# A new written order for the first ten cells: x's low parts copied between the halves by ScalarE, masks of five weight units in PSUM

## The chip, the cores and the metric

The kernel runs on one NeuronCore of one Trainium2 chip. The metric is device microseconds from the start to the end of one execution. Before the change three runs gave a median of 1227.36 us; two of them lie at 1226.69 and 1227.36, the third at 2097.7.

## The reference, cut to what matters

```python
# x: (2, 4096, 192), weight_gen: (2, 4096, 8, 7); all float32
w = softmax(weight_gen, axis=-1)                 # 7 weights for each token and head
out[b, s, h, g] = sum_k w[b, s, h, k] * x_pad[b, s + k, h, g]   # causal window of 7 tokens
x = out.reshape(8192, 192)
h = x @ w_in1;  x = where(h > 0, h, exp(min(h, 0)) - 1) @ w_out1    # 192 -> 2048 -> 192
h = x @ w_in2;  x = (h * clip(h + 3, 0, 6) / 6) @ w_out2            # 192 -> 2048 -> 192
```

All inputs are float32, and the products are made nearly exact: each operand is split into a high part (`h`) and a low rest (`l`), and three products of parts are added (high by high, high by low, low by high).

## The kernel before, in words

**Tiling.** The 8192 tokens are 16 blocks of 512. A cell is one block, one of the two layers and one eighth of the 2048 hidden columns, so a block has 8 cells per layer, and the kernel 256 cells in all. A cell n has a first product (18 pairs of matmuls with 64 rows each, into two of the four `h` banks of PSUM: `h00` and `h01` for even n, `h10` and `h11` for odd n), an activation on ScalarE (`act_a`, L556 and L557), a gate on VectorE (`gate`, L573), the rounding of the result to `gh` on ScalarE (L563), its rest `gl` on VectorE (L567), and a second product, which is issued with the first product of cell n + 3 into `acca` and `accb`. All matmuls of cells are recorded at L536.

**Weight units.** The weights of layer one are split on the chip, in 16 units of 384 columns (numbered 0 to 15; units 4, 6, 8, 10 and 12 to 15 belong to `w_out`, the others to `w_in`). A unit takes a mask step on ScalarE (`B`, L158), five integer steps on VectorE (`s0` to `s4` at L162, L165, L169, L174, L185, written C9.0 to C9.4 for unit 9), a rounding to the high part on ScalarE (`H`, L180), three matmuls that make the low part in a PSUM bank (`P`, L191 to L193), and the copy of that bank into the low weights (`L`, L198). The strings `masks` and `sums` name, per unit, where the steps' scratch lies and into which bank the three matmuls go: `x` is `aux`, `b` is `accb`, `a` and `c` are the two `acca`, `d` to `g` the banks `h00`, `h01`, `h10`, `h11`, and `-` an SBUF tile called `tr`.

**The window products.** The window sum of a block is made on GpSimd (`attention`, L290 and L299): 14 tensor operations on SBUF of about 1.5 to 2.7 us. They start when VectorE has scaled the block's softmax weights (L278).

**The written order.** Up to cell 9 nothing is scheduled by rule: the instructions are issued in the order of the string `SCRIPT`, and each engine executes its own in that order. `M3` there is the matmuls of cell 3, `x3` and `y3` the activations of its two banks, `X3` and `Y3` their gates, `R3` and `G3` the two rounding steps. `s1a`, `e1`, `s1b`, `s1c` and `sA`, `sE`, `sB`, `sC` are the softmax steps of blocks 1 and 2, the last of each with L278 and GpSimd's products behind it. `T1`, `J` and `j` transpose and split x of block 1. For block 0, `wh0` and `wh1` round x to `xh`, `wh2` and `wh3` copy `xh` between the partition halves on ScalarE (L348), and `wl0` and `wl1` make the rest `xl` on VectorE (L352). `wl1` also issues two DMAs on SyncE's queue that copy `xl` between the halves (L357), and then the loads of units 8 to 11. From cell 10 on, the loop at the end of the kernel sets the order, with a stream that spreads the weight units of layer two over the cells.

Of the kernel before, what the change touches and what calls it, by code (L numbers as in the profile page):

```python
# [8 lines left out]
F32 = mybir.dt.float32  # L9
# [8 lines left out]
def kernel(  # L18
# [20 lines left out]
    nc = tc.nc  # L39
# [19 lines left out]
    half = slice(0, HP), slice(HP, P)  # L59
# [268 lines left out]
    def prepare(m, i):  # L328
        X = xts[m, i] = {
            k: act.tile([P, 2, XN], F32R, tag=f"x{k}", name=f"x{k}") for k in "hl"}  # L330
        v = lambda t: t[:, 0].rearrange("p (h c) -> p h c", h=2)
        if m == 0:

            y, yd = ya.pop(i)
            ps = acca if i == 0 else (acca[i % 2], aux)
            for t, src in enumerate([y[:, t, 0:P] for t in range(TM)] + [yd[:, s] for s in range(2)]):
                for h, p in enumerate(half):
                    nc.tensor.transpose(ps[h][:, t * HP:(t + 1) * HP], src[p], ident[p, p])  # L338
            parts = [(ps[h][:, 0:XN // 2], (lambda h: lambda t: v(t)[:, h])(h)) for h in range(2)]
        else:  # L340
            parts = [(zin.pop(i)[:, 0:XN], lambda t: t[:, 0])]

        def cast(k):
            src, w = parts[k]
            nc.scalar.copy(w(X["h"]), src)  # L345

        def turn(a):
            nc.scalar.copy(X["h"][half[1 - a], 1], X["h"][half[a], 0].bitcast(F32))  # L348

        def rest(k):  # L350
            src, w = parts[k]
            nc.vector.tensor_tensor(w(X["l"]), src, w(X["h"]).bitcast(F32), op=ALU.subtract)  # L352

        def swap(keys, put):
            for k in keys:
                for a in range(2):
                    put(X[k][half[1 - a], 1].bitcast(F32), X[k][half[a], 0].bitcast(F32))  # L357

        def split():
            for k in range(len(parts)):  # L360
                cast(k)
            for k in range(len(parts)):
                rest(k)
            swap("hl", lambda o, t: later(1 if (m, i) == (0, 2) else 2, o, t))
        split.cast, split.turn, split.rest, split.swap = cast, turn, rest, swap
        return split

# [227 lines left out]
    def later(n, out, in_):  # L595

        if now is None or now >= len(cells) or now < BOOT and n == 0:
            nc.sync.dma_start(out, in_)
        else:
            waiting.append((now + n, out, in_))  # L600
# [8 lines left out]
    class Stream:  # L609
# [21 lines left out]
    BOOT = 10  # L631
    units = [(u[0], 0, int(u[1]), k) for k, u in enumerate("i0 i1 i2 i3 o0 i4 o1 i5 o2 i6 o3 i7 o4 o5 o6 o7".split())]
    banks = {"x": aux, "b": accb, "a": acca[0], "c": acca[1], "d": hset[0][0], "e": hset[0][1], "f": hset[1][0], "g": hset[1][1]}
    masks, sums = "xxbaccxcx----ccc", "xxbfbedgfedxcxxx"
    made = {}
    SCRIPT = """
        s1a B2 B1 C2.0 e1 C1.0 wh0 s1b wh1 wh2 wl0 s1c wh3 wl1 C2.1 B4 M0 C1.1 B3 C2.2 C4.0 H2 C1.2 C4.1 H1
        C1.3 C3.0 C1.4 C4.2 P1 x0 C3.1 C4.3 C3.2 L1 M1 C4.4 y0 C2.3 X0 B5 C2.4 B6 Y0 P2 x1 C5.0 C6.0 y1 C3.3
        C6.1 X1 L2 M2 H3 C3.4 R0 Y1 C5.1 P3 H4 C6.2 x2 G0 P4 y2 C5.2 C6.3 L3 C5.3 L4 M3 C6.4 C5.4 X2 B7 B8
        Y2 R1 C8.0 C7.0 H5 C8.1 H6 P5 C7.1 x3 C8.2 G1 P6 L5 B9 B10 C7.2 L6 M4 C8.3 H7 sA C10.0 sE X3 y3 C7.3  # L640
        C10.1 C9.0 H8 C8.4 R2 C7.4 Y3 P7 x4 C9.1 C10.2 P8 C9.2 L7 G2 H10 T1 L8 C10.3 y4 M5 C9.3 X4 C9.4 J
        C10.4 sB B12 H9 j B11 R3 Y4 P9 B13 sC C11.0 C12.0 G3 P10 L9 x5 C11.1 C12.1 C11.2 L10 M6 C13.0 H11
        C12.2 C13.1 H12 C11.3 x6 C13.2 C11.4 C13.3 R4 C12.3 C13.4 P11 y5 C12.4 X5 P12 G4 H13 L11 L12 Y5 B14
        X6 M7 R5 C14.0 C14.1 x7 G5 y6 X7 C14.2 P13 H14 C14.3 Y6 L13 M8 C14.4 y7 R6 Y7 B15 G6 x8 P14 R7 C15.0
        X8 L14 M9 C15.1 C15.2 H15 C15.3 C15.4 x9 G7 y8 P15 y9 Y8 X9 L15 Y9 R8 G8
    """

    groups = [("io"[n % 2], 1, n // 2) for n in range(2 * NQ)]
# [22 lines left out]
    with tc.manual_schedule():  # L671
        nc.vector.memset(three, 3.0)
        nc.scalar.activation(warm, three, AF.Exp)
        def make(k):
            made[k] = Unit(*units[k])
# [20 lines left out]
        c1, split = attention(1), {0: prepare(0, 0)}  # L696
# [29 lines left out]
        def special(t):  # L726
            if t == "T1":
                split[1] = prepare(0, 1)
            elif t in ("s1a", "e1", "s1b"):
                c1.pop(0)()  # L730
            elif t == "s1c":
                for s in c1:
                    s()
            elif t == "J":
                split[1].cast(0)
                split[1].cast(1)
            elif t == "j":
                split[1].rest(0)
                split[1].rest(1)
                split[1].swap("hl", nc.sync.dma_start)  # L740
            elif t[:2] == "wh":
                k = int(t[2])
                (split[0].turn if k > 1 else split[0].cast)(k % 2)
            elif t[:2] == "wl":
                split[0].rest(int(t[2]))
                if t == "wl1":
                    split[0].swap("l", nc.sync.dma_start)
                    for k in range(8, RAWS + 8):
                        make(k)
            else:  # L750
                if t == "sA":
                    softmax[2] = attention(2)
                softmax[2].pop(0)()
# [6 lines left out]
        for t in SCRIPT.split():  # L760
            if t[0] == "C":
                k, p = t[1:].split(".")
                getattr(made[int(k)], "s" + p)()
            elif t[0] in plain and t[1:].isdigit():
                plain[t[0]](int(t[1:]))
            else:
                special(t)
# [65 lines left out]
```

## Time and profile before

| | us |
|---|---|
| median of the runs | 1227.36 |
| the profiled execution's own time | 1227.44 |
| its span, first to last instruction | 1225.6 |
| TensorE busy | 1188.1 (97%) |
| VectorE busy | 944.3 (77%) |
| ScalarE busy | 856.4 (70%) |
| GpSimd busy | 417.6 (34%) |

The profiled execution is 0.08 us above the median. An engine's busy share is a mean over the whole span; the page's second part cuts the span into 40 slices of 30.6 us and gives each in tenths. The timelines start from the first instruction of the span.

### The profile page before, as it was taken

The numbers are of one execution on the slowest core, as the hardware profiler recorded it, in microseconds if no ns is written. First come the engines' busy times: TensorE is split into PE (matmuls) and PEld (weight loads), VectorE is DVE, ScalarE is ACT, GpSimd is POOL, SyncE is SP. The second block draws the span as 40 slices with busy tenths as digits, with TensorE's granted clock in tenths as the row PEclk, the third lists the DMA queues.
The fourth block names the chain that finished last, engine by engine and source line by source line (L and its number), as shares of the span: only waits on it lengthen the run. The fifth ranks groups of instructions, "written<-read, shape, count | busy, mean of one in ns | idle before, by whom it ended". The sixth has DMA issues, their size and how long they took to land.

```text
span 1225.6 us, 25362 instructions
## 1 busy us (share of the span) xinstructions
PE 1188.1 (97%) x10146; PEld 941.7 (77%) x10146; DVE 944.3 (77%) x1223; ACT 856.4 (70%) x1339; POOL 417.6 (34%) x234
## 2 busy tenths in 40 slices
PE   2979999999999999999999999999999999999998
PEld 1647787777778777778788888888888888888886
DVE  7897999999999999998777666666666666666664
ACT  3858788888888888888886666556665555666654
POOL 7582778777778877777000000000000000000000
PEclk9989999999999999999999999999999999999999
DMA  9421122221122222121121111111101111111110
GB/s 207 120 63 62 40 88 89 89 79 65 39 83 89 89 88 69 41 68 53 54 64 52 28 40 53 52 40 53 46 27 46 53 53 40 53 36 30 53 40 27
DMA packets 33414, 75.42 MB, mean 62 GB/s; under 512 B 4372, under 2 KB 17042, under 8 KB 33296
## 3 DMA queue, kind: packets, MB, share of 16 engines
q1 hardware_dynamic: 33152, 73.60, 21.0%
q8 instruction: 80, 1.31, 0.5%
q14 instruction: 38, 0.31, 0.1%
q10 hardware_dynamic: 144, 0.20, 0.0%
HBM read 36.43 MB, written 12.58 MB: 40 GB/s over the span
## 4 chain that ended last, share of the span: by engine, by line
PE 91%; DVE 2%; ACT 0%; DMA 0%; issue 0%; SPq 0%
PE h L536 42%; PE acca L536 28%; PE accb L536 19%; DVE gl L567 1%; PE acca L338 1%; PE acca L432 0%; DVE r L573 0%; PE acca L504 0%; DVE boot L185 0%; PE accb L504 0%; DVE tr L174 0%; DMA xl<-xl 0%; ACT gh L563 0%; PE aux L191 0%; DVE tr L185 0%
## 5 line engine op out<-in xcount | busy, mean ns | idle before, releaser
L536 PE MATMUL h<-xl,wi_h 64*128 64x512 f32 x1536 | 563.2, 395 | 4.4 <-DMA xl<-xl 4.4
L536 PE MATMUL h<-xh,wi_h 64*128 64x512 f32 x1536 | 565.3, 396 | 2.0 <-ACT xh L345 1.5
L536 PE MATMUL h<-xh,wi_l 64*128 64x512 f32 x1536 | 567.1, 396 | 0.1
L536 PE MATMUL acca<-gh,wo 64*128 64x512 f32 x2024 | 558.3, 394 | 0.1
L567 DVE TENSOR_TENSOR gl<-r,gh 128x1024 fp32r<-128x1024 f32 x256 | 394.3, 1540 | 62.7 <-ACT gh L563 61.6
L536 PEld LDWEIGHTS acca<-gh,wo 64*128 64x128 f32 x2024 | 373.5, 185 | 48.5 <-issue 1.6
L559 ACT ACTIVATE r<-h,three 128x512 f32<-128x512 f32 x256 | 176.3, 689 | 222.2 <-PE h L536 112.4
L536 PE MATMUL accb<-gh,wo 64*128 64x512 f32 x1012 | 319.9, 395 | 0.6 <-ACT wo L198 0.6
L536 PE MATMUL acca<-gl,wo 64*128 64x512 f32 x1012 | 317.8, 393 | 1.3 <-DVE gl L567 1.2
L536 PE MATMUL accb<-gl,wo 64*128 64x512 f32 x1012 | 317.3, 393 | 0.3 <-DVE gl L567 0.3
L536 PEld LDWEIGHTS h<-xl,wi_h 64*128 64x128 f32 x1536 | 282.8, 186 | 40.1 <-DMA xl<-xl 5.1
L536 PEld LDWEIGHTS h<-xh,wi_h 64*128 64x128 f32 x1536 | 283.0, 186 | 38.9 <-ACT xh L345 1.7
L536 PEld LDWEIGHTS h<-xh,wi_l 64*128 64x128 f32 x1536 | 282.9, 186 | 35.4 <-ACT wi_l L198 0.5
L576 DVE SCALAR_TENSOR_TENSOR r<-r,h 128x512 f32<-128x512 f32 x256 | 175.8, 687 | 161.1 <-ACT r L559 160.1
L563 ACT CAST gh<-r 128x1024 fp32r<-128x1024 f32 x256 | 266.6, 1042 | 13.3 <-DVE r L573 12.5
L536 PEld LDWEIGHTS acca<-gl,wo 64*128 64x128 f32 x1012 | 186.9, 185 | 26.0 <-DVE gl L567 2.8
L536 PEld LDWEIGHTS accb<-gl,wo 64*128 64x128 f32 x1012 | 186.9, 185 | 23.8 <-DVE gl L567 0.8
L573 DVE SCALAR_TENSOR_TENSOR r<-r,h 128x512 f32<-128x512 f32 x256 | 172.9, 676 | 37.5 <-ACT r L557 36.6
L536 PEld LDWEIGHTS accb<-gh,wo 64*128 64x128 f32 x1012 | 185.0, 185 | 21.6 <-ACT wo L198 0.9
L290 POOL TENSOR_TENSOR tmp<-xt,wt 128x768 f32<-128x768 f32 (+1 forms) x95 | 189.8, 1998 | 6.2
L556 ACT ACTIVATE r<-h 128x512 f32<-128x512 f32 x256 | 152.7, 596 | 49.6 <-PE acca L536 29.0
L557 ACT ACTIVATE r<-r 128x512 f32<-128x512 f32 x256 | 162.0, 633 | 8.1
(158 smaller groups left out, 757.5 us busy)
## 6 DMA issues: line engine op xcount, KB each, us to landing
xt<-in_x_dram SPq DMA_DIRECT2D x14, 960.0 KB, 5.7
xl<-xl SPq DMA_DIRECT2D x64, 192.0 KB, 2.9
xh<-xh SPq DMA_DIRECT2D x62, 192.0 KB, 2.7
z<-z SPq DMA_DIRECT2D x16, 384.0 KB, 2.3
zin<-z SPq DMA_DIRECT2D x16, 384.0 KB, 3.0
out_dram<-ot SPq DMA_DIRECT2D x15, 384.0 KB, 2.3
raw<-in_moe_w_out_dram SPq DMA_DIRECT2D x12, 384.0 KB, 3.1
raw<-in_moe_w_in_dram SPq DMA_DIRECT2D x12, 192.0 KB, 3.4
```

What stands on the lines that cost most here:

```text
L290: eng.tensor_tensor(o.rearrange("p t (h g) -> p t h g", g=G), xk, wk.rearrange("p (t h) g -> p t h g", h=H), op=ALU.mult)
L338: nc.tensor.transpose(ps[h][:, t * HP:(t + 1) * HP], src[p], ident[p, p])
L536: mm = nc.tensor.matmul(o, w, r, start=st, stop=sp).ins
L556: nc.scalar.activation(r, h, AF.Relu, scale=-1.0)
L557: nc.scalar.activation(r, r, AF.Exp, scale=-1.0)
L559: nc.scalar.activation(r, h, AF.Relu, bias=three)
L563: nc.scalar.copy(gg[n][0], rs[n])
L567: nc.vector.tensor_tensor(gl, rs.pop(n), gh.bitcast(F32), op=ALU.subtract)
L573: nc.vector.scalar_tensor_tensor(r, r, -1.0, h, op0=ALU.add, op1=ALU.max)
L576: nc.vector.scalar_tensor_tensor(r, r, 6.0, h, op0=ALU.min, op1=ALU.mult)
```

## The change

Three things are done. The copy of block 0's `xl` between the halves is no longer two DMAs: `turn` takes the part as an argument, and two new words of the script, `wz0` and `wz1`, let ScalarE copy it, as it already does with `xh`. The scratch of units 11 to 15 is `x`, `c`, `x`, `c`, `x` (before: `tr`, `tr`, `c`, `c`, `c`), so only units 9 and 10 keep `tr`, and the sums of units 11 to 15 go to `g`, `f`, `d`, `f`, `d`, the `h` banks (before: `x`, `c`, `x`, `x`, `x`). The string `SCRIPT` is written anew from its second line on.

```diff
-        def turn(a):
-            nc.scalar.copy(X["h"][half[1 - a], 1], X["h"][half[a], 0].bitcast(F32))
+        def turn(a, k="h"):
+            nc.scalar.copy(X[k][half[1 - a], 1], X[k][half[a], 0].bitcast(F32))
...
-    masks, sums = "xxbaccxcx----ccc", "xxbfbedgfedxcxxx"
+    masks, sums = "xxbaccxcx--xcxcx", "xxbfbedgfedgfdfd"
...
-        s1a B2 B1 C2.0 e1 C1.0 wh0 s1b wh1 wh2 wl0 s1c wh3 wl1 C2.1 B4 M0 C1.1 B3 C2.2 C4.0 H2 C1.2 C4.1 H1
...
-        Y2 R1 C8.0 C7.0 H5 C8.1 H6 P5 C7.1 x3 C8.2 G1 P6 L5 B9 B10 C7.2 L6 M4 C8.3 H7 sA C10.0 sE X3 y3 C7.3
-        C10.1 C9.0 H8 C8.4 R2 C7.4 Y3 P7 x4 C9.1 C10.2 P8 C9.2 L7 G2 H10 T1 L8 C10.3 y4 M5 C9.3 X4 C9.4 J
-        C10.4 sB B12 H9 j B11 R3 Y4 P9 B13 sC C11.0 C12.0 G3 P10 L9 x5 C11.1 C12.1 C11.2 L10 M6 C13.0 H11
...
+        s1a B2 B1 C2.0 e1 C1.0 wh0 s1b wh1 wh2 wl0 s1c wh3 C1.1 wl1 C2.1 B3 C1.2 wz0 C3.0 C2.2 B4 C1.3 wz1
+        M0 C2.3 H1 C4.0 H2 C3.1 C4.1 x0 C1.4 C4.2 P1 C3.2 C4.3 C3.3 L1 M1 C4.4 B6 X0 B5 H3 C5.0 y0 C6.0 C5.1
+        C2.4 x1 Y0 P2 C6.1 y1 X1 C5.2 R0 C6.2 C5.3 C3.4 L2 M2 Y1 H4 H6 G0 P3 x2 P4 y2 C6.3 C5.4 L3 X2 L4 M3
...
+        C10.0 C7.4 C9.0 C10.1 C9.1 x4 C10.2 C9.2 Y3 H8 sE C8.3 H10 P7 X4 R3 C8.4 G2 P8 L7 sB T1 L8 M5 J
+        C10.3 C9.3 sC y4 C9.4 j H9 G3 B12 B11 x5 C11.0 C10.4 Y4 P9 C12.0 P10 L9 C11.1 R4 C12.1 C11.2 C12.2
+        L10 M6 C11.3 y5 C12.3 C11.4 H11 X5 B13 Y5 x6 C12.4 C13.0 H12 P11 G4 B14 P12 L11 R5 C13.1 X6 L12 M7
...
+            elif t[:2] == "wz":
+                split[0].turn(int(t[2]), "l")
             elif t[:2] == "wl":
                 split[0].rest(int(t[2]))
                 if t == "wl1":
-                    split[0].swap("l", nc.sync.dma_start)
                     for k in range(8, RAWS + 8):
                         make(k)
```

What the new string does to the engines' own orders is seen in three places. The first is ScalarE, from the copies of block 0's `xh` to the activations of cell 0 (`r<-h_73` is x0, `r<-h_72` is y0).

```order
 L348 CAST xh<-xh 64x768 x2
+L158 ACTIVATE acca_76<-raw 128x384
+L348 CAST xl<-xl 64x768
 L158 ACTIVATE acca_77<-early_h 128x384
-L158 ACTIVATE acca_76<-raw 128x384
+L348 CAST xl<-xl 64x768
 L180 CAST wi_h<-f 128x384 x2
 L556 ACTIVATE r<-h_73 128x512
 L557 ACTIVATE r<-r 128x512
 L198 CAST wi_l<-aux 128x384
```

The two copies of `xl` stand here between the mask steps of units 3 and 4, ahead of everything that belongs to cell 0; further down the masks of units 6 and 5 and the high part of unit 3 now stand ahead of y0.

The second place is VectorE, from the last softmax step of block 2 (L278) on, before the change:

```order
L573 SCALAR_TENSOR_TENSOR r<-r,h_72 128x512
L278 TENSOR_TENSOR wt<-wt,mx 128x224
L162 TENSOR_SCALAR tr<-tr 128x384 x2
L567 TENSOR_TENSOR gl<-r,gh 128x1024
L165 TENSOR_SCALAR tr<-tr 128x384 x2
L169 SCALAR_TENSOR_TENSOR f<-early_l,tr 128x384
L162 TENSOR_SCALAR acca_77<-acca_77 128x384
L169 SCALAR_TENSOR_TENSOR f<-raw,tr 128x384
L165 TENSOR_SCALAR acca_77<-acca_77 128x384
L174 TENSOR_SCALAR tr<-f 128x384
```

and from the same step on with the change:

```order
L278 TENSOR_TENSOR wt<-wt,mx 128x224
L185 SCALAR_TENSOR_TENSOR boot<-early_l,tr 128x384
L352 TENSOR_TENSOR xl<-acca_77,xh 128x384
L352 TENSOR_TENSOR xl<-aux,xh 128x384
L567 TENSOR_TENSOR gl<-r,gh 128x1024
L162 TENSOR_SCALAR aux<-aux 128x384
L185 SCALAR_TENSOR_TENSOR boot<-early_l,tr 128x384
L573 SCALAR_TENSOR_TENSOR r<-r,h_72 128x512
L162 TENSOR_SCALAR acca_77<-acca_77 128x384
L165 TENSOR_SCALAR aux<-aux 128x384
```

Before, the gate Y4 (`r<-r,h_72`) stood ahead of L278 and units 11 and 12 followed it in `tr`; now the last steps of units 9 and 10, the rests of x of block 1 and G3 stand between L278 and Y4, and the units behind it lie in `aux` and `acca`.

The third place is TensorE between the cells 6 and 7, where the three matmuls of units 11 and 12 stand, before the change:

```order
L536 MATMUL accb<-gl,wo_89 128x512
L191 MATMUL aux<-f,ident 128x384
L192 MATMUL aux<-wi_h,minus 128x384
L193 MATMUL aux<-boot,plus 128x384
L191 MATMUL acca_77<-f,ident 128x384
L192 MATMUL acca_77<-wo_89,minus 128x384
L193 MATMUL acca_77<-boot,plus 128x384
```

and with the change:

```order
L536 MATMUL accb<-gl,wo_89 128x512
L191 MATMUL h_75<-f,ident 128x384
L192 MATMUL h_75<-wi_h,minus 128x384
L193 MATMUL h_75<-boot,plus 128x384
L191 MATMUL h_74<-f,ident 128x384
L192 MATMUL h_74<-wo_89,minus 128x384
L193 MATMUL h_74<-boot,plus 128x384
```

The place in TensorE's order is the same; the sums now go into the two banks (`h_75` is h11, `h_74` is h10) that the gates of cell 5 read.

## Rows read from the trace of the kernel before

**Rows 1.** The page's second part: the span in 40 slices, two lines.

```profile
PE   2979999999999999999999999999999999999998
PEclk9989999999999999999999999999999999999999
```

**Rows 2.** Timeline of TensorE: start, us, engine, line, operation, tiles [idle before].

```profile
30.65 1.22 PE L536 MATMUL h<-xl,wi_h 64*128 64x512 f32 x4 [4.42 <-DMA xl<-xl]
...
42.75 0.50 PE L536 MATMUL acca<-gh,wo 64*128 64x512 f32 x1
...
57.63 0.47 PE L536 MATMUL acca<-gh,wo 64*128 64x512 f32 x1
...
62.26 0.91 PE L191 MATMUL h<-f,ident 128*128 128x384 f32 x2
...
64.45 0.50 PE L536 MATMUL acca<-gh,wo 64*128 64x512 f32 x1
...
76.89 0.69 PE L193 MATMUL aux<-boot,plus 128*128 128x384 f32 x1 [4.71 <-DVE boot L185]
78.97 1.65 PE L191 MATMUL acca<-f,ident 128*128 128x384 f32 x2 [1.39 <-DVE boot L185]
...
81.22 0.79 PE L536 MATMUL acca<-gh,wo 64*128 64x512 f32 x1
...
88.90 0.50 PE L536 MATMUL acca<-gh,wo 64*128 64x512 f32 x1
...
94.74 0.50 PE L536 MATMUL acca<-gh,wo 64*128 64x512 f32 x1
...
101.27 0.49 PE L536 MATMUL accb<-gh,wo 64*128 64x512 f32 x1 [0.63 <-ACT wo L198]
```

**Rows 3.** Timeline of VectorE, 62 to 82 us, around GpSimd's start.

```profile
62.57 0.62 DVE L162 TENSOR_SCALAR tr<-tr 128x384 f32<-128x384 f32 x2
63.11 2.57 DVE L567 TENSOR_TENSOR gl<-r,gh 128x1024 fp32r<-128x1024 f32 x1
65.59 3.62 DVE L165 TENSOR_SCALAR tr<-tr 128x384 uint32<-128x384 uint32 x2
...
73.04 0.55 DVE L165 TENSOR_SCALAR acca<-acca 128x384 uint32<-128x384 uint32 x1
...
75.13 1.71 DVE L185 SCALAR_TENSOR_TENSOR boot<-early_l,tr 128x384 fp32r<-128x384 uint32 x1
...
81.06 1.96 DVE L567 TENSOR_TENSOR gl<-r,gh 128x1024 fp32r<-128x1024 f32 x1
```

**Rows 4.** Timeline of VectorE, 56 to 60 us, GpSimd idle.

```profile
56.69 1.22 DVE L567 TENSOR_TENSOR gl<-r,gh 128x1024 fp32r<-128x1024 f32 x1
57.83 0.62 DVE L174 TENSOR_SCALAR tr<-f 128x384 uint32<-128x384 uint32 x2
58.37 0.68 DVE L573 SCALAR_TENSOR_TENSOR r<-r,h 128x512 f32<-128x512 f32 x1
58.96 1.02 DVE L185 SCALAR_TENSOR_TENSOR boot<-early_l,tr 128x384 fp32r<-128x384 uint32 x2
```

**Rows 5.** Timeline of GpSimd: the first product of block 2.

```profile
62.87 1.72 POOL L290 TENSOR_TENSOR y<-xt,wt 128x768 f32<-128x768 f32 x1 [15.89 <-PE accb L536]
```

**Rows 6.** Timeline of ScalarE, 22 to 32 us.

```profile
22.01 1.67 ACT L348 CAST xh<-xh 64x768 fp32r<-64x768 f32 x2
...
31.92 0.60 ACT L556 ACTIVATE r<-h 128x512 f32<-128x512 f32 x1 [5.44 <-PE h L536]
```

**Rows 7.** Timeline of VectorE, 22 to 34 us.

```profile
22.36 0.49 DVE L352 TENSOR_TENSOR xl<-acca,xh 128x384 fp32r<-128x384 f32 x1
...
26.32 0.55 DVE L174 TENSOR_SCALAR aux<-f 128x384 uint32<-128x384 uint32 x1
26.78 0.55 DVE L162 TENSOR_SCALAR acca<-acca 128x384 f32<-128x384 f32 x1
...
33.21 0.69 DVE L573 SCALAR_TENSOR_TENSOR r<-r,h 128x512 f32<-128x512 f32 x1 [2.63 <-ACT r L557]
```

More of the change, by code (lines that the diff above doesn't have):

```diff
@@ L633 @@
     banks = {"x": aux, "b": accb, "a": acca[0], "c": acca[1], "d": hset[0][0], "e": hset[0][1], "f": hset[1][0], "g": hset[1][1]}
-    masks, sums = "xxbaccxcx----ccc", "xxbfbedgfedxcxxx"
+    masks, sums = "xxbaccxcx--xcxcx", "xxbfbedgfedgfdfd"
     made = {}
     SCRIPT = """
-        s1a B2 B1 C2.0 e1 C1.0 wh0 s1b wh1 wh2 wl0 s1c wh3 wl1 C2.1 B4 M0 C1.1 B3 C2.2 C4.0 H2 C1.2 C4.1 H1
-        C1.3 C3.0 C1.4 C4.2 P1 x0 C3.1 C4.3 C3.2 L1 M1 C4.4 y0 C2.3 X0 B5 C2.4 B6 Y0 P2 x1 C5.0 C6.0 y1 C3.3
-        C6.1 X1 L2 M2 H3 C3.4 R0 Y1 C5.1 P3 H4 C6.2 x2 G0 P4 y2 C5.2 C6.3 L3 C5.3 L4 M3 C6.4 C5.4 X2 B7 B8
-        Y2 R1 C8.0 C7.0 H5 C8.1 H6 P5 C7.1 x3 C8.2 G1 P6 L5 B9 B10 C7.2 L6 M4 C8.3 H7 sA C10.0 sE X3 y3 C7.3
-        C10.1 C9.0 H8 C8.4 R2 C7.4 Y3 P7 x4 C9.1 C10.2 P8 C9.2 L7 G2 H10 T1 L8 C10.3 y4 M5 C9.3 X4 C9.4 J
-        C10.4 sB B12 H9 j B11 R3 Y4 P9 B13 sC C11.0 C12.0 G3 P10 L9 x5 C11.1 C12.1 C11.2 L10 M6 C13.0 H11
-        C12.2 C13.1 H12 C11.3 x6 C13.2 C11.4 C13.3 R4 C12.3 C13.4 P11 y5 C12.4 X5 P12 G4 H13 L11 L12 Y5 B14
-        X6 M7 R5 C14.0 C14.1 x7 G5 y6 X7 C14.2 P13 H14 C14.3 Y6 L13 M8 C14.4 y7 R6 Y7 B15 G6 x8 P14 R7 C15.0
-        X8 L14 M9 C15.1 C15.2 H15 C15.3 C15.4 x9 G7 y8 P15 y9 Y8 X9 L15 Y9 R8 G8
+        s1a B2 B1 C2.0 e1 C1.0 wh0 s1b wh1 wh2 wl0 s1c wh3 C1.1 wl1 C2.1 B3 C1.2 wz0 C3.0 C2.2 B4 C1.3 wz1
+        M0 C2.3 H1 C4.0 H2 C3.1 C4.1 x0 C1.4 C4.2 P1 C3.2 C4.3 C3.3 L1 M1 C4.4 B6 X0 B5 H3 C5.0 y0 C6.0 C5.1
+        C2.4 x1 Y0 P2 C6.1 y1 X1 C5.2 R0 C6.2 C5.3 C3.4 L2 M2 Y1 H4 H6 G0 P3 x2 P4 y2 C6.3 C5.4 L3 X2 L4 M3
+        H5 C6.4 B7 Y2 B8 sA R1 C7.0 C8.0 B10 C7.1 x3 P5 C8.1 C7.2 y3 X3 P6 G1 L5 L6 B9 H7 C7.3 M4 R2 C8.2
+        C10.0 C7.4 C9.0 C10.1 C9.1 x4 C10.2 C9.2 Y3 H8 sE C8.3 H10 P7 X4 R3 C8.4 G2 P8 L7 sB T1 L8 M5 J
+        C10.3 C9.3 sC y4 C9.4 j H9 G3 B12 B11 x5 C11.0 C10.4 Y4 P9 C12.0 P10 L9 C11.1 R4 C12.1 C11.2 C12.2
+        L10 M6 C11.3 y5 C12.3 C11.4 H11 X5 B13 Y5 x6 C12.4 C13.0 H12 P11 G4 B14 P12 L11 R5 C13.1 X6 L12 M7
+        y6 C13.2 C14.0 C13.3 x7 Y6 C13.4 H13 G5 P13 y7 C14.1 L13 X7 M8 B15 R6 C14.2 Y7 x8 C14.3 C15.0 C14.4
+        H14 G6 P14 y8 C15.1 L14 X8 M9 R7 C15.2 C15.3 Y8 x9 C15.4 G7 H15 P15 y9 X9 L15 Y9 R8 G8
     """
```

## The prediction

> **What bounds the kernel now.** I read the page's slices first, then the timelines of the first 105 us, one engine after the other. The slices [rows 1] show TensorE at nine tenths from the fourth slice to the last but one: from 101.27 us on [rows 2], where cell 10 begins, nothing but TensorE's own work sets the end, and the 1225.6 - 101.27 = 1124.3 us behind it are the loop that the change doesn't touch. Only the part that the script writes, the first 101 us, can move. TensorE has two holes there [rows 2]: 4.42 us before 30.65, waiting for the DMA of `xl`, and the stretch from the end of cell 6's matmuls near 70 to the start of cell 7 at 81.22, with 4.71 and 1.39 us of waiting for the step `boot` of units 11 and 12 on VectorE.
>
> The second hole is explained by VectorE and GpSimd together [rows 3, 4, 5]. While GpSimd is idle, a step in `tr` takes 0.27 us to the next start (57.83 to 58.37 for two), the last step 0.5, and G 1.14. After GpSimd has begun block 2 at 62.87, the pair of `tr` steps takes 3.62, the last step 1.71 and G 2.57 or 1.96. A step in `acca` takes 0.55 at 73.04, in the middle of it, and 0.46 from start to start, the same as at 26.32 to 26.78 [rows 3, 7].
>
> **The change, part by part. The copies of `xl`.** Two copies of 64x768 on ScalarE cost 1.67 us together [rows 6]. ScalarE ends the copies of `xh` at 23.7; mask, copy, mask, copy (0.46 + 0.83 twice) bring `xl` at 26.3, where the DMA brought it at 30.65. They cost the path nothing beyond that: ScalarE was idle for 5.44 us before 31.92 [rows 6]. If that cover were gone, 1.67 us would be late on x0. The DMAs removed from SyncE's queue stood in front of the loads of units 8 to 11, which come earlier for it and were not waited for.
>
> So TensorE no longer stops there, but what comes next is VectorE's queue. It was idle for 2.63 us before 33.21 [rows 7] and no longer is. From 22.36 it has 24 instructions before the gate Y0, at 0.46 each: Y0 starts at 33.4. ScalarE agrees with it: the mask of unit 5 now waits for the last step of unit 4 on VectorE (19 instructions, 31.1), and behind it on ScalarE stand H3 and y0, 0.46 + 0.4 + 1.2, so y0 is done at 33.2. That wait is hidden by VectorE's own queue. Behind Y0 come one step, X1, four steps (0.6 + 0.46 + 0.6 + 1.84, 0.1 of waiting for x1) and Y1 at 37.0, done at 37.65. Cell 2's matmuls end at about the same time, since they need L2, which ScalarE reaches after x1, y1 and R0 at 36.6. Units 3 and 4 take 2.2 on TensorE (62.26 to 64.45 for two units, rows 2), and cell 3 starts at 39.95, where it started at 42.75 [rows 2]: 2.8 us earlier.
>
> **Cells 3 to 5** have the same TensorE order before and after, and the waits that I followed there (G0, L4, G1, Y3, G2) each end before TensorE comes to them or within 0.1 us. From cell 3 to the units 9 and 10 it was 62.26 - 42.75 = 19.5 us; unit 9 adds 1.1, so TensorE is through with unit 9 at 39.95 + 19.5 + 1.1 = 60.55.
>
> **Unit 10 adds a wait.** Its sum goes into h00, so the gate Y4 must have read it. VectorE's queue from Y1 at 37.0 to the last softmax step of block 2: six gates at 0.6 (58.37 to 58.96, rows 4) are 3.6; G0 beside GpSimd's first block, at the mean of the two rows less the overlap, 2.2, and G1 and G2 without it 1.14 each, 4.5; 13 steps in PSUM at 0.46, 6.0; six in `tr` at 0.27 and two at 0.5, 2.6; six small softmax steps taken like the short `tr` step, 0.3 each, 1.8. Together 18.5, so the last of them ends at 55.5, and GpSimd's block 2 starts there, 7 us earlier than before. Then come the last step of unit 9, two rests of x at 0.46, G3, one step in `aux`, the last step of unit 10, and Y4. Unit 9's step I take as free, 0.5, since the first two `tr` steps after L278 took 0.62 together [rows 3]; G3 beside GpSimd is 2.2, unit 10's step 1.7: 0.5 + 0.9 + 2.2 + 0.46 + 1.7 + 0.65 = 6.4, plus 0.3 for a G1 that may still meet the end of GpSimd's first block. Y4 ends at 62.2. TensorE waits 1.65 us, takes unit 10 in 1.1 and starts cell 6 at 63.3, where it started at 64.45. Most of the early gain is spent here: behind it on TensorE stands all of cell 6, and ScalarE's R4 waits for the same gate.
>
> The bounds of this term: with both `tr` steps free and G at 1.96, Y4 is there before 60.6 and cell 6 starts at 61.65; with unit 9's step at 1.7, G at 2.5 twice and G1 at 1.9 like the others, 2.6 us later, at 65.9. The values taken lie between because GpSimd starts within this stretch, not before it.
>
> The Trainium skill, page "SBUF — State Buffer", section "SBUF: two separate sides", says that VectorE and GpSimd lock a port pair for a whole instruction, so a VectorE step with two SBUF inputs waits for what is left of GpSimd's instruction and no more. By that, unit 10's step may cost anything from 0.5 to 2.0 us, and the sum would come out at 1213.3 to 1214.8; the rows above show the longer waits and can't tell a share from a lock.
>
> **Cells 6 to 9.** Units 11 to 15 now have their scratch in PSUM, where a step is 0.46 beside GpSimd [rows 3, 7]. With GpSimd idle this costs 0.2 us for a step that was 0.27, which is not the case here. From Y4 on VectorE needs ten steps, two gates and G4 (4.6 + 1.2 + 2.2 = 8.0) and has G4 at 70.2. Cell 6 and two units take TensorE 64.45 - 57.63 = 6.8 [rows 2], so cell 7 starts at 70.1 and needs G4 two pairs later, 70.7. Then five steps, two gates and G each time, 5.7 us: G5 at 75.9 and G6 at 81.6. TensorE takes 94.74 - 88.90 = 5.84 for a cell and one unit: cell 8 starts at 75.95, cell 9 at 81.8, each about 0.7 before it would meet its G. The last goes with 101.27 - 94.74 = 6.5, its wait for L15 included: cell 10 starts at 88.3.
>
> **Sum.** 101.27 - 88.3 = 12.95 us less. The profiled execution took 1227.44, 0.08 above the median, so 1227.44 - 12.95 = 1214.5 us. In parts: 2.8 from the start, 1.65 lost at Y4, and the rest, 11.8, from the hole of units 11 and 12.
>
> **Rivals.** First, the wait at Y4 is long enough to lose the clock. After the 4.71 us of waiting at 76.89 the units ran slowly: 2.25 us for unit 12 (78.97 to 81.22) against 1.1, and 0.79 against 0.50 for the first matmul of the cell [rows 2]: 1.2 GHz in place of 2.4, as the granted clock of that slice, eight tenths, also says [rows 1]. That is 1.15 + 2 x 0.3 = 1.75 us on top: 1216.3, or 1218.9 with the upper bound of the wait. For it speaks that I have 1.65 to 4.3 us of idling there, against it that the short one of 0.63 before 101.27 left the first matmul at 0.49 [rows 2]. The Trainium skill, page "TensorE: Matmul & The Clock Gate", section "What's actually happening", makes the slow clock the default state that a spell of idling brings back; the trace agrees after 4.71 us, and no row shows a gap between the two.
>
> Second, PSUM does not shield: the steps write `f` and `boot` and read the raw weights in SBUF, and could be held up too. Then the second hole stays and only the start's 2.8 us are left: 1224.6. Against it stands the 0.55 at 73.04 between two delayed ones [rows 3].
>
> Third, the other side: the sums in the `h` banks make every unit from 11 on wait for a gate (X5 and Y5, Y6, Y7, Y8), as unit 10 does for Y4. If VectorE falls behind, each of the four places stops TensorE like the hole at 76.89 and starts it slowly, 4.71 + 1.75 = 6.5, 25.8 in all: 1214.5 + 25.8 = 1240.3. It decides from 12.95 / 4 = 3.2 us for a place, which is 1.5 of waiting and the slow clock behind it. The margin of 0.7 us that I find at each place speaks against it; that VectorE has no idle time in my walk from Y0 to G6 speaks for it.
>
> **Numbers.** The forecast gets 0.66, the slow clock 0.2, no shield 0.08, the waits at the banks 0.06. The likeliest time is 1214.5. The range takes the bounds of the wait at Y4 (cell 6 at 61.65 or 65.9: 1212.9 to 1217.1) and the slow clock behind it, and some of the way to the second rival: 1212 to 1221. About 2% is what a measurement of this kernel can tell from no change, some 24.5 us: a gain of that size would need more than the holes hold (0.01), and a loss of it nearly twice the third rival (0.02); within it 0.97.
>
> **What would show it.** Right: no DMA before the last matmuls of cell 0, and they start near 26.4; cell 3 at 40, cell 6 at 63.3 after a wait for VectorE of one to three microseconds; GpSimd's block 2 from 55.5 to 56; steps of units 11 to 15 at 0.55 beside it; cell 10 near 88.3, and an unchanged stretch behind. Wrong: matmuls of the units at 2.2 us, steps in `aux` over 1 us, waits for L573 before units 11 to 15, or cell 10 to the end longer than 1124.3.

## The result, and the profile after

The changed kernel takes 1214.11 us (median of four runs, 1213.14 to 1214.77), the kernel before, on the same chip, 1227.67: a ratio of 0.9891 (95% interval 0.9872 to 0.9911). Predicted were 1214.5 us, 1212 to 1221, and a difference within 2%. The measured time lies in the range, 0.4 us from the likeliest; the difference is small, but its interval ends below 1, so it is a gain. The 1227.67 is a median of four runs, of which one took 2097.7 us; the ratio leaves that run out. The profiled execution took 1213.52 us, its span is 1211.7.

The page's slices, which answer to [rows 1]:

```profile
PE   3899999999999999999999999999999999999998
PEclk9999999999999999999999999999999999999999
```

TensorE stands at nine tenths from the third slice to the last but one, and the slice with a granted clock of eight tenths is gone. The timeline of TensorE, to be read beside [rows 2]:

```profile
25.67 0.74 PE L536 MATMUL h<-xl,wi_h 64*128 64x512 f32 x4 [0.19 <-ACT xl L348]
27.71 0.91 PE L191 MATMUL aux<-f,ident 128*128 128x384 f32 x2 [1.31 <-DVE boot L185]
...
32.56 0.91 PE L191 MATMUL accb<-f,ident 128*128 128x384 f32 x2 [1.30 <-DVE boot L185]
...
38.87 0.50 PE L536 MATMUL acca<-gh,wo 64*128 64x512 f32 x1
...
47.16 0.49 PE L536 MATMUL acca<-gl,wo 64*128 64x512 f32 x1 [0.64 <-DVE gl L567]
...
60.86 0.91 PE L191 MATMUL h<-f,ident 128*128 128x384 f32 x2 [1.07 <-DVE r L573]
...
62.04 0.49 PE L536 MATMUL acca<-gh,wo 64*128 64x512 f32 x1
...
68.88 0.50 PE L536 MATMUL acca<-gh,wo 64*128 64x512 f32 x1
...
75.17 0.49 PE L536 MATMUL acca<-gh,wo 64*128 64x512 f32 x1
...
81.01 0.50 PE L536 MATMUL acca<-gh,wo 64*128 64x512 f32 x1
...
87.55 0.50 PE L536 MATMUL accb<-gh,wo 64*128 64x512 f32 x1 [0.63 <-ACT wo L198]
```

Both holes of before are closed: the last matmuls of cell 0 wait 0.19 us for ScalarE where they waited 4.42 for a DMA, and nothing stops TensorE between 62.04 and 75.17. Three waits of over a microsecond are new, all of them for VectorE: 1.31 and 1.30 us in the opening, before the units 1 and 2, for the step `boot`, and 1.07 us before unit 10, for the gate Y4. Cell 10 starts 13.72 us earlier than at 101.27, and from there to the end it is 1211.7 - 87.55 = 1124.15 us (before 1124.33).

VectorE and GpSimd around GpSimd's start, to be read beside [rows 3] and [rows 5]. VectorE:

```profile
55.05 0.39 DVE L278 TENSOR_TENSOR wt<-wt,mx 128x224 f32<-128x224 f32 x1
55.35 0.55 DVE L185 SCALAR_TENSOR_TENSOR boot<-early_l,tr 128x384 fp32r<-128x384 uint32 x1
...
56.75 1.64 DVE L567 TENSOR_TENSOR gl<-r,gh 128x1024 fp32r<-128x1024 f32 x1
...
58.78 1.42 DVE L185 SCALAR_TENSOR_TENSOR boot<-early_l,tr 128x384 fp32r<-128x384 uint32 x1
60.13 0.67 DVE L573 SCALAR_TENSOR_TENSOR r<-r,h 128x512 f32<-128x512 f32 x1
...
61.20 0.55 DVE L165 TENSOR_SCALAR aux<-aux 128x384 uint32<-128x384 uint32 x1
...
72.12 2.36 DVE L567 TENSOR_TENSOR gl<-r,gh 128x1024 fp32r<-128x1024 f32 x1
```

GpSimd:

```profile
55.66 1.65 POOL L290 TENSOR_TENSOR y<-xt,wt 128x768 f32<-128x768 f32 x1 [9.63 <-PE acca L536]
57.27 2.52 POOL L290 TENSOR_TENSOR tmp<-xt,wt 128x768 f32<-128x768 f32 x1
```

GpSimd works from 55.66 to 82.8. Within that time a step in `aux` takes 0.55 us, and what has both operands in SBUF is drawn out: unit 10's last step in `tr` 1.42, G 1.64 and 2.36. The two copies on ScalarE, between those of `xh` and the activations of cell 0, a stretch with 5.44 us of idle time before [rows 6]:

```profile
23.49 0.83 ACT L348 CAST xl<-xl 64x768 fp32r<-64x768 f32 x1
...
24.78 0.83 ACT L348 CAST xl<-xl 64x768 fp32r<-64x768 f32 x1
```

The program's opening varies from run to run by more than some of the differences below: the first rest of x (L352, 22.36 in [rows 7]) starts between 20.95 and 22.68 in the profiled executions, and at 21.30 here. The stretch behind it varies too: the changed kernel was profiled three times, and cell 3 starts 17.57 us after the first rest in the trace above, 18.55 and 19.75 in the two others, where the matmuls of unit 1 run at half speed (1.65 us for its first pair, 0.91 above). Places in two traces are therefore compared from that rest, or from the start of a cell, and times by their ratio to the kernel before on the same chip.

### The profile page after: what moved, and what is told of

The parts are those of the page before. It is cut to its first block, busy times and chain, and to the rows that moved or that the text cites. A ratio compares the mean times of both kernels' runs of the same rounds, so it can differ in the third digit from the quotient of the medians.

```text
span 1211.7 us, 25367 instructions
## 1 busy us (share of the span) xinstructions
PE 1183.4 (98%) x10146; PEld 944.5 (78%) x10146; DVE 936.2 (77%) x1223; ACT 857.6 (71%) x1341; POOL 418.1 (35%) x234
## 3 DMA queue, kind: packets, MB, share of 16 engines
q8 instruction: 80, 1.31, 0.5%
## 4 chain that ended last, share of the span: by engine, by line
PE 93%; DVE 4%; DMA 1%; SPq 1%; ACT 0%; issue 0%; DVEq 0%; ACTq 0%
PE h L536 43%; PE acca L536 29%; PE accb L536 19%; DVE gl L567 1%; DVE r L573 1%; DMA xt<-in_x_dram 1%; SPq L598 1%; PE acca L338 1%; PE acca L432 0%; DVE boot L185 0%; PE acca L504 0%; PE h L191 0%; DVE f L169 0%; DMA early_h<-in_moe_w_out_dram 0%; PE accb L504 0%
```

## The experiments

### Each part without the other

**The new order, with the DMAs of `xl` kept.**

```diff
-        ... B3 C1.2 wz0 C3.0 C2.2 B4 C1.3 wz1
+        ... B3 C1.2 C3.0 C2.2 B4 C1.3
                 if t == "wl1":
+                    split[0].swap("l", nc.sync.dma_start)
```

> The changed kernel with one thing undone: xl of block 0 is again copied by two DMAs, issued behind the rests; the order is otherwise the new one. My theory: the DMAs land some 8.3 us after the first rest (as before: 22.36 to 30.65), 4 us later than the copies; the first gate X0 on VectorE is reached 3 us late, VectorE is the bound up to Y4, and all of it comes out at the end: 1216.5 to 1218. Rival: the wait at Y4 and the margins behind it hide the transfer, and the copies are worth nothing by now: 1214 to 1215.

Measured: 1217.69 us (1217.01 to 1217.96), ratio 0.9912 (0.9894 to 0.9931). TensorE of this kernel:

```profile
29.72 1.22 PE L536 MATMUL h<-xl,wi_h 64*128 64x512 f32 x4 [3.87 <-DMA xl<-xl]
...
64.68 0.91 PE L191 MATMUL h<-f,ident 128*128 128x384 f32 x2 [1.07 <-DVE r L573]
```

The first hole is back and the wait at Y4 is as long as without it: the delay goes through VectorE's queue to the end. Cell 10 starts 69.41 us after the first rest, with the copies 66.25, 66.27 and 67.40 in the three traces. So the copies are worth 2 to 3 us within the new order.

**The old order, with the copies on ScalarE.** The words stand between the masks of units 4 and 3.

```diff
-        ... wl1 C2.1 B4 M0 C1.1 B3 C2.2 ...
+        ... wl1 C2.1 B4 wz0 C1.1 B3 wz1 M0 C2.2 ...
```

> The kernel before with one part of the change alone: xl of block 0 is copied by ScalarE, between the masks of units 4 and 3; nothing else is moved. My theory: VectorE loses its 4.1 us of idle time before 36 us, and since it is the bound up to the hole, the hole opens 3 to 4 us earlier with its size unchanged: 1223.5 to 1225. Rival: the hole is set by GpSimd's block 2, which starts behind TensorE's transposes, and takes the gain back: 1226 to 1228.

Measured: 1224.56 us (1222.25 to 1225.44), ratio 0.9964 (0.9949 to 0.9979): the copies' part alone. TensorE of this kernel:

```profile
25.81 1.22 PE L536 MATMUL h<-xl,wi_h 64*128 64x512 f32 x4 [0.36 <-ACT xl L348]
...
72.94 0.69 PE L193 MATMUL aux<-boot,plus 128*128 128x384 f32 x1 [4.71 <-DVE boot L185]
75.03 1.65 PE L191 MATMUL acca<-f,ident 128*128 128x384 f32 x2 [1.40 <-DVE boot L185]
```

The second hole stays as it was, 4.71 and 1.40 us, and with it the units at half speed (1.65 us for the pair).

**The old order, with units 11 and 12 in PSUM.** Unit 13 is moved behind unit 12, since they share a bank; the DMAs stay.

```diff
-    masks, sums = "xxbaccxcx----ccc", "xxbfbedgfedxcxxx"
+    masks, sums = "xxbaccxcx--xcccc", "xxbfbedgfedxcxxx"
...
-        C10.4 sB B12 H9 j B11 R3 Y4 P9 B13 sC C11.0 C12.0 G3 ...
+        C10.4 sB H9 j B12 B11 R3 Y4 P9 sC C11.0 C12.0 G3 ...
```

> The kernel before with the other part alone: the scratch of units 11 and 12 in aux and acca. Since acca is then taken, the masks of units 12 and 11 stand behind the rests of x of block 1, and unit 13 (same bank) goes behind unit 12's copy; the DMAs of xl and the sums stay as they were. My theory: the hole of 11 us before cell 7 falls to 2 us or less, some of it comes back as later steps of unit 13: 1218 to 1221. Rival: without the earlier start of VectorE the steps still come too late, and the hole keeps more than half: 1222 to 1226.

Measured: 1217.63 us (1216.14 to 1218.88), ratio 0.9912 (0.9893 to 0.993), a little less than the range expected. TensorE of this kernel, units 11 and 12:

```profile
67.30 0.91 PE L191 MATMUL aux<-f,ident 128*128 128x384 f32 x2
...
68.40 0.81 PE L191 MATMUL acca<-f,ident 128*128 128x384 f32 x2
```

Neither waits, and neither is slow. The hole goes with the scratch alone, in the old order too.

**The old order, with both parts.** The two edits above together.

> The order before with both parts: xl copied by ScalarE and units 11 and 12 in PSUM (unit 13 behind unit 12, the sums in the old banks). My theory: the two parts add, since the first moves VectorE's queue and the second shortens it: 3.8 + 10.7 = 14.5 less than before, 1213.5 to 1215, so the rest of the new order and the h banks are worth nothing by themselves. Rival: with the hole gone TensorE is the bound and the start's gain is lost in the waits for L15 and G6 that the moved unit 13 brought: 1216 to 1218.

Measured: 1215.28 us (1214.04 to 1216.21), ratio 0.9887 (0.9872 to 0.9902). That is the ratio of the change, 0.9891: the copies (0.9964) and the scratch (0.9912) give 0.9876 as a product, and what else the new order moves is worth nothing that these runs can tell. What is left on TensorE in this kernel lies elsewhere than in the changed one: 1.72 us before cell 10, where the changed kernel waits 0.63.

### The scratch taken out of PSUM again

**The new order with units 11 and 12 in an SBUF tile of their own (`ts`)**, the sums still in the `h` banks.

```diff
-    masks, sums = "xxbaccxcx--xcxcx", "xxbfbedgfedgfdfd"
+    masks, sums = "xxbaccxcx--ttxcx", "xxbfbedgfedgfdfd"
```

> The changed kernel with one thing undone: the scratch of units 11 and 12 lies in an SBUF tile of its own (two buffers), not in aux and acca; the order is the new one. My theory: the ten steps of these two units run beside GpSimd's block 2, where the rows of before show 1.0 to 1.9 us in place of 0.46, so VectorE loses 9 to 11 us before G4, the units' matmuls wait for the step boot, TensorE falls to the slow clock there, and the time is 1223 to 1226. Rival: the new order, which starts GpSimd and the units earlier, fills the hole by itself, and PSUM is worth little: 1214 to 1217.

Measured: 1227.05 us (1226.14 to 1228.03), ratio 0.9991 (0.9982 to 1.0001). The whole gain is gone, the opening's too, which I had expected to remain. VectorE of this kernel:

```profile
59.60 2.16 DVE L185 SCALAR_TENSOR_TENSOR boot<-early_l,tr 128x384 fp32r<-128x384 uint32 x1
...
63.30 3.60 DVE L165 TENSOR_SCALAR ts<-ts 128x384 uint32<-128x384 uint32 x2
```

and TensorE:

```profile
62.41 1.65 PE L191 MATMUL h<-f,ident 128*128 128x384 f32 x2 [2.79 <-DVE r L573]
...
64.63 0.79 PE L536 MATMUL acca<-gh,wo 64*128 64x512 f32 x1
...
77.07 1.65 PE L191 MATMUL h<-f,ident 128*128 128x384 f32 x2 [5.95 <-DVE r L573]
...
81.21 0.79 PE L536 MATMUL acca<-gh,wo 64*128 64x512 f32 x1
```

Beside GpSimd a pair of steps in `ts` takes 3.6 us and a single one mostly 1.7 to 2.2; a step in PSUM takes 0.46 from start to start. The ten steps of the two units are spread over 20 us. TensorE now waits 2.79 us for Y4, before unit 10, and 5.95 us for a gate of cell 5, before unit 11, and it begins slowly each time. The second hole is back at its old size: cell 6 to cell 7 takes 81.21 - 64.63 = 16.58 us, before 81.22 - 64.45 = 16.77. What uses up the opening's gain is the wait before unit 10 and the slow start behind it: cell 3 to cell 6 takes 64.63 - 39.58 = 25.05 us, before 21.70. A step in `ts` of 1.70 us and the 2.16 us of unit 10's last step stand ahead of Y4. So it is the prediction's first rival, the wait at Y4 that loses the clock, that came here. Of the third, the gates ahead of the sums from unit 11 on, there is little: the gate that unit 11 waits for ends near 77.0, and the step `boot` that the unit needs anyway ends at 76.41.

### The wait before unit 10

**Y4 alone moved earlier,** ahead of G3.

```diff
-        C10.3 C9.3 sC y4 C9.4 j H9 G3 B12 B11 x5 C11.0 C10.4 Y4 P9 ...
+        C10.3 C9.3 sC y4 C9.4 j Y4 H9 G3 B12 B11 x5 C11.0 C10.4 P9 ...
```

> The changed kernel with the gate Y4 moved ahead on VectorE, from behind unit 10's last step to directly behind the rests of x of block 1 (its activation is done at 56.2 there), so that unit 10's sum need not wait for it. My theory: the 1.07 us of waiting on TensorE before unit 10 go, cell 6 starts 0.7 to 1.1 us earlier against the first gate, VectorE has G4 and G5 just in time, and the time is 1212.8 to 1213.6. Rival: G3, unit 10's last step and G4 come later on VectorE by the 0.6 of the gate, and the waits only change their place: 1213.8 to 1214.4.

Measured: 1214.72 us (1214.35 to 1215.19), ratio 0.9883 (0.9869 to 0.9898): no gain. VectorE of this kernel:

```profile
57.51 2.56 DVE L567 TENSOR_TENSOR gl<-r,gh 128x1024 fp32r<-128x1024 f32 x1
...
60.46 1.70 DVE L185 SCALAR_TENSOR_TENSOR boot<-early_l,tr 128x384 fp32r<-128x384 uint32 x1
```

GpSimd:

```profile
57.44 1.55 POOL L290 TENSOR_TENSOR tmp<-xt,wt 128x768 f32<-128x768 f32 x1
59.07 2.67 POOL L299 TENSOR_TENSOR y<-y,tmp 128x768 f32<-128x768 f32 x1
```

and TensorE:

```profile
62.22 0.44 PE L193 MATMUL h<-boot,plus 128*128 128x384 f32 x1 [1.32 <-DVE boot L185]
```

The wait went from the unit's first matmul to its third, which needs unit 10's last step. Both that step and G3 got longer, 1.70 and 2.56 us in place of 1.42 and 1.64: G3 now starts 0.07 us after GpSimd's second instruction and ends only when that one is over. The gate was the last of a late queue, not its cause.

**Y4 moved later,** behind five steps in PSUM, to see whether a longer wait loses the clock.

```diff
-        ... x5 C11.0 C10.4 Y4 P9 C12.0 P10 L9 C11.1 R4 C12.1 C11.2 C12.2
+        ... x5 C11.0 C10.4 C12.0 C11.1 C12.1 C11.2 C12.2 Y4 P9 P10 L9 R4
```

> The changed kernel with Y4 five PSUM steps later on VectorE (2.3 us), so TensorE idles some 3.4 us before unit 10 in place of 1.07. If a gap of that size brings the slow clock, as the 2.8 us of the run with SBUF scratch seem to show, unit 10 takes 2.2 us and the first pairs of cell 6 0.6: 2.3 + 1.8 = 4.1 us late at cell 6, less what VectorE's unchanged queue gives back nowhere, since TensorE is then the bound: 1217 to 1218.5. If the clock stays, only the 2.3 us are lost: 1215.8 to 1216.8.

Measured: 1218.72 us (1216.08 to 1219.27), ratio 0.9917 (0.9901 to 0.9934). The profiled execution is the shortest of the four, 1216.08 us at a mean granted clock of 0.999. It lies in the range that I gave for a clock that stays, and its TensorE shows the full clock after the gap:

```profile
63.42 0.91 PE L191 MATMUL h<-f,ident 128*128 128x384 f32 x2 [3.28 <-DVE r L573]
```

The other three took 1218.28 to 1219.27 us at 0.997 to 0.998. So the same wait leaves the clock full in one run, and three runs are 2.2 to 3.2 us longer at a lower clock; that they lost it at this place was not seen, as they have no trace. In the kernel with `ts` a shorter gap, 2.79 us, was followed by slow matmuls. Windows of TensorE from 57 us on, columns busy time and count of PE, PEld, DVE, ACT and POOL, then the granted clock, in the kernel with `ts`:

```profile
57.00:66.00 9.00, 6.21 (x28) 3.83 (x26) 9.00 (x7) 4.18 (x9) 8.69 (x5) 0.76 0.59 170
```

and in this one:

```profile
57.00:70.00 13.00, 9.72 (x67) 6.67 (x63) 11.88 (x18) 7.91 (x16) 12.53 (x8) 1.00 0.48 146
```

0.76 against 1.00. So the length of the gap alone does not tell which; what does was not found. The Trainium skill, page "TensorE: Matmul & The Clock Gate", section "What's actually happening", says that the chip's watch on TensorE's activity runs on a time of its own, not from the kernel's start, so that the outcome may differ from run to run. The four runs agree with it, and no run here shows it by itself.

**The late instructions moved ahead of GpSimd's start.** If GpSimd's work draws them out, the cure is not to move the gate but to let GpSimd begin behind them.

```diff
-        C10.3 C9.3 sC y4 C9.4 j H9 G3 B12 B11 x5 C11.0 C10.4 Y4 P9 ...
+        C10.3 C9.3 y4 C9.4 C10.4 H9 G3 Y4 sC j B12 B11 x5 C11.0 P9 ...
```

> The changed kernel, but the last softmax step of block 2, which lets GpSimd begin, stands behind the last steps of units 9 and 10, G3 and the gate Y4 on VectorE. Theory (what Y4 waits for is the time that GpSimd takes from the instructions ahead of it; the earlier trial that moved Y4 alone left those beside GpSimd): the last steps of units 9 and 10 take 0.5 each and G3 1.14 to 1.2, as with GpSimd idle, Y4 is done near 57.8 where it was done at 60.8, TensorE goes from unit 9 to unit 10 without waiting, and cells 6 to 10 start about 1.1 us earlier against the first rest of x: 1.0 to 1.2 us less than the changed kernel measured beside it. GpSimd's block 2 begins near 58.3 in place of 55.7, which nothing waits for. Rival 1: the microsecond only moves on, to a wait of cell 7 for G4 or of cell 10 for the low weights of unit 15: within 0.3 us of the changed kernel. Rival 2: TensorE's wait at this place came from somewhere else than VectorE's late steps: a wait of 1 us stays before unit 10.

> The changed kernel again, for the comparison with the version beside it on the same chip: 1213.5 to 1215, ratio 0.988 to 0.990.

Measured: 1213.28 us (1212.82 to 1214.14), ratio 0.9868 (0.9853 to 0.9882); the changed kernel beside it 1214.35 (1213.51 to 1214.97), 0.9873 (0.9857 to 0.989). The medians differ by 1.07 us, as expected, but the runs of the two overlap. VectorE of the new version:

```profile
54.95 1.03 DVE L185 SCALAR_TENSOR_TENSOR boot<-early_l,tr 128x384 fp32r<-128x384 uint32 x2
55.90 1.22 DVE L567 TENSOR_TENSOR gl<-r,gh 128x1024 fp32r<-128x1024 f32 x1
57.03 0.68 DVE L573 SCALAR_TENSOR_TENSOR r<-r,h 128x512 f32<-128x512 f32 x1
```

its TensorE, unit 10 and the cells 6 and 7:

```profile
59.41 0.81 PE L191 MATMUL h<-f,ident 128*128 128x384 f32 x2
...
60.49 0.50 PE L536 MATMUL acca<-gh,wo 64*128 64x512 f32 x1
61.10 0.49 PE L536 MATMUL h<-xh,wi_h 64*128 64x512 f32 x1
...
68.22 0.50 PE L536 MATMUL acca<-gh,wo 64*128 64x512 f32 x1
```

and its ScalarE:

```profile
58.52 0.54 ACT L158 ACTIVATE acca<-raw 128x384 f32<-128x384 f32 x1 [2.17 <-DVE xl L352]
```

The theory holds for the instructions: G3 takes 1.22 us in place of 1.64, the two last steps 1.03 together, Y4 is done at 57.7, and unit 10 does not wait. Cell 3 to cell 6 takes 60.49 - 38.68 = 21.81 us (23.17 in the changed kernel's trace shown above, where cell 3 starts as long after the first rest). But cell 6 to cell 7 takes 7.73 in place of 6.84: ScalarE stood 2.17 us for the rests of x of block 1, which now came late and whose banks the masks of units 11 and 12 overwrite, and the copies of the low parts of units 9 and 10 behind those masks kept cell 6 from its banks. Of 1.36 us gained 0.89 went back within one cell.

**The rests of x ahead of GpSimd's start as well.**

```diff
-        C10.3 C9.3 y4 C9.4 C10.4 H9 G3 Y4 sC j B12 ...
+        C10.3 C9.3 y4 C9.4 C10.4 j H9 G3 Y4 sC B12 ...
```

> The version before (last steps of units 9 and 10, G3 and Y4 ahead of the softmax step that lets GpSimd begin), with the two rests of x of block 1 ahead of G3 as well. In that version the wait before unit 10 was gone, but ScalarE stood idle for 2.17 us for those rests, since the masks of units 11 and 12 go into the banks that they read, and the copies of the low parts of units 9 and 10 behind them came late: cell 6 to cell 7 took 7.73 us where the changed kernel takes 6.84. Theory (those 0.89 us are the delayed masks): ScalarE's masks begin near 56.5 again, cell 6 to cell 7 takes 6.8 to 6.9, no wait before unit 10, and cell 10 starts 64.8 to 65.1 us after the first rest of x (changed kernel 66.25, version before 65.8): 1.1 to 1.6 us less than the changed kernel measured beside it. Rival: ScalarE's own queue (mask, mask, x5, low part of unit 9, R4, low part of unit 10) is the limit: cell 6 to cell 7 stays over 7.4, and the gain is 0.4 to 0.8.

> The changed kernel, for the comparison on the same chip: ratio 0.987 to 0.990.

Measured: 1212.83 us (1211.87 to 1213.64), ratio 0.9874 (0.9858 to 0.9891); the changed kernel beside it 1214.26 (1213.87 to 1214.91), 0.9889 (0.9874 to 0.9904). The four runs of the one all lie below the four of the other; the medians differ by 1.43 us, 0.1%, which lies in the range expected. TensorE of the new version:

```profile
41.25 0.50 PE L536 MATMUL acca<-gh,wo 64*128 64x512 f32 x1
...
61.12 0.81 PE L191 MATMUL h<-f,ident 128*128 128x384 f32 x2
...
62.21 0.50 PE L536 MATMUL acca<-gh,wo 64*128 64x512 f32 x1
...
69.04 0.50 PE L536 MATMUL acca<-gh,wo 64*128 64x512 f32 x1
```

Cell 6 to cell 7 takes 6.83 us again, as the theory of the delayed masks had it. My number for cell 10, 64.8 to 65.1 us after the first rest, was missed: it is 87.73 - 21.57 = 66.16. The reason is the opening, where unit 1 ran at half speed in this execution (1.65 us for its first pair, as in most of the traces) and cell 3 started only 41.25 - 21.57 = 19.68 us after the first rest. The changed kernel's trace beside it had lost less there (18.55), so the two do not show the gain. The changed kernel's trace taken with the version before had lost as much (cell 3 at 41.38 - 21.63 = 19.75):

```profile
41.38 0.50 PE L536 MATMUL acca<-gh,wo 64*128 64x512 f32 x1
...
63.50 0.49 PE L536 MATMUL acca<-gh,wo 64*128 64x512 f32 x1
```

Against it cell 3 to cell 6 takes 20.96 us in place of 22.12, and cell 10 starts 66.16 us after the first rest in place of 67.40: 1.24 us, in the range expected. That this version is faster than the one before it is not shown: the ratios are 0.9874 and 0.9868, measured on two chips, and their intervals overlap.

## Why the prediction was right, step by step

Against the profiled execution the steps give this (before minus after, us):

| stretch | predicted | measured |
|---|---|---|
| first rest of x itself | 0 | 1.06 |
| first rest to cell 3 | 2.8 | 20.39 - 17.57 = 2.82 |
| cell 3 to cell 6 | -1.65 | 21.70 - 23.17 = -1.47 |
| cell 6 to cell 10 | 11.8 | 36.82 - 25.51 = 11.31 |
| cell 10 to the end | 0 | 1124.33 - 1124.15 = 0.18 |

The sum is 13.9, the difference of the spans; 12.95 was predicted.

**The opening** was right for the execution shown: VectorE's queue behind the new `xl`, not the copies, sets Y1 and with it cell 3. VectorE shows no idle time from the first rest to Y1, as its queue of steps was counted, Y1 starts 35.94 - 21.30 = 14.64 us after the first rest (forecast 37.0 - 22.36 = 14.64), and TensorE waits 1.31 and 1.30 us for VectorE on the way. L2 on ScalarE comes at nearly the same time as Y1, as the prediction said: TensorE waits 0.35 us for it before unit 3. (The forecast's own terms, 37.65 + 2.2, give 39.85 for cell 3 and not 39.95.) That this run began 1.06 us earlier is no part of the change; without it the steps give 12.8. There is luck in the 2.8, too: in the two other traces of the changed kernel unit 1 ran at half speed, VectorE had idle time before Y1, and cell 3 came only 1.8 and 0.6 us earlier than before against the first rest. The prediction looked for slow matmuls at Y4 alone. The late cell 3 cost the end 1.15 us at most: cell 10 starts 66.25, 66.27 and 67.40 us after the first rest in the three traces (forecast 88.3 - 22.36 = 65.94).

**Cell 3 to cell 6** came right by misses that cancel. The prediction had VectorE take 18.5 us from Y1 to the last softmax step; it took 55.44 - 35.94 = 19.5, mostly because G1 met the end of GpSimd's first block (1.63 us to the next start, taken as 1.14) and the six small softmax steps took 2.3 us in place of 1.8. From there to the end of Y4 it took 5.4 and not 6.7, because G3 and unit 10's step were held up less (1.64 and 1.42, taken as 2.2 and 1.7); the 0.3 in the 6.7 was kept for G1, which took more and took it earlier. So the wait before unit 10 was 1.07 and not 1.65. And G1, which I had ready within 0.1 us, let TensorE wait 0.64 at 47.16. Two of the three traces of the changed kernel put Y4 at 60.13 - 21.30 and 61.51 - 22.68, both 38.83 us after the first rest, though cell 3 started 17.57 and 18.55 after it: there it is VectorE's queue that keeps the time, as the prediction said. In the third, with cell 3 at 19.75, Y4 starts at 61.58 - 21.63 = 39.95, so a still later opening is passed on.

**The shield** was right, and it is the main term: 0.55 us for a step in PSUM beside GpSimd [rows 3], about 1.8 with the scratch put back into SBUF, and then no gain at all. The prediction's second rival priced that case at 1224.6; the run gave a ratio of 0.9991, some 1226.3, and its trace has the slow start behind the longer wait at Y4 on top. A step or a G beside GpSimd has no fixed price: 1.42 and 1.70 for the same last step of unit 10, 1.64 and 2.56 for the same G3, in two orders that differ in one gate. What sets the price can be read from the ends. G3 ends 1.08 us after the end of a GpSimd instruction in the changed kernel (57.31 and 58.39), and G in the kernel before 1.09 us after one (64.59 and 65.68 [rows 3, 5]); unit 10's last step ends 0.41 us after one (59.79 and 60.20), and 0.42 with Y4 moved earlier (61.74 and 62.16). So each waits for the end of GpSimd's instruction and then takes about as long as with GpSimd idle. The Trainium skill, page "SBUF — State Buffer", section "SBUF: two separate sides", says the same: of a GpSimd instruction and a VectorE instruction with two SBUF inputs, the one that starts first has the shared ports for its whole length, and the other waits. The ends agree with such a lock; a share of the ports, which would slow both at once, would not put them there. No run was made to test it.

**Cells 6 to 10** were 0.5 us longer than predicted, and one step of it was mis-sized: cell 7 with its unit takes 75.17 - 68.88 = 6.29 us, not the 5.84 of cell 8, because it carries two matmuls more (40 against 38 in the trace), of 0.23 us each. The margins held: no wait for G4 to G6.

**The slow clock** (0.2) did not come at Y4: the pair of unit 10 behind the wait of 1.07 us took 0.91. It was no empty rival, though: at 2.79 us it came, at 3.28 it stayed away once. For a gap between 0.63 and 4.71 us, of which the prediction says that no row shows one, the trace of the kernel before had this line, full speed behind 1.12 us:

```profile
71.09 0.91 PE L191 MATMUL aux<-f,ident 128*128 128x384 f32 x2 [1.12 <-DVE f L169]
```

## What to carry to other kernels

Where a second engine works in SBUF, move the short steps that a third engine waits for into PSUM, or ahead of the point at which that engine is let loose; moving only the instruction that is waited for moves the wait. When such a move costs another engine's start (here the masks that reuse a bank), that engine's queue takes part of the gain back a microsecond later, so look at who writes next what the moved instruction reads. And compare traces from a common event, and only those whose stretch before it went alike, since the opening here drifts by more than the last edits are worth.

## What the runs showed of the hardware that was not expected

A gap in TensorE's work does not fix the clock behind it by its length: the unit's pair of matmuls took 1.65 us after 2.79 us of waiting and 0.91 after 3.28, in the same place of the program. The first pair of unit 1, early in the program, took 1.65 us with no wait just ahead of it in four kernels, whose last matmuls of cell 0 had waited 4.42 us (before), 3.87 (new order with the DMAs), 2.93 (old order with PSUM) and 0.36 (old order with the copies). In one and the same kernel, the changed one, it took 0.91 us behind a wait of 1.31 in one trace and 1.65 behind waits of 1.12 and 0.75 in the two others. The granted clock reads 1.00 in that stretch in all these traces, so that the early slow pairs ran at the lower clock is concluded from their length alone.

The same step on VectorE, with GpSimd at work, cost 1.42, 1.70 and 2.16 us in three orders (unit 10's last step, in `tr`); with its scratch in PSUM a step cost 0.53 to 0.57 wherever it stood.
